# Attention and two expert layers on one core: a rewritten opening of the first batch, and attention work of every second step put ahead of the value product

## The chip, the cores and the metric

The kernel runs on one core of a Trainium2 chip. Its engines are TensorE (PE in the profile; its weight loads are PEld), VectorE (DVE), ScalarE (ACT), GpSimd (POOL) and SyncE (SP, which here issues nearly all DMAs). Each engine carries out its own instructions in the order in which the program writes them. The metric is device time in microseconds of one execution.

## The reference, cut to what matters

```python
# attention between x [8, 8, 512, 64] and state [8, 8, 32, 64], each way
a = softmax(x @ state.T / 8);   xread = a @ state      # 512 rows a batch
a2 = softmax(state @ x.T / 8);  sread = a2 @ x         # 32 rows a batch
x = rows of (xread, sread), heads side by side         # 4352 rows of 512
# gated layer
xn = x / sqrt(mean(x * x) + 1e-6) * rms_g
x = (silu(xn @ w_gate) * (xn @ w_val)) @ w_out         # 512 -> 1536 -> 512
# routed layer: rows with x @ w_skip > 0 go to the best of 8 experts
x[do] += gate * (relu(x[do] @ w1[e]) @ w2[e])          # 512 -> 1024 -> 512
```

## The kernel before, in words

**Passes and steps.** The gated layer runs in nine passes `b` over the rows: passes 0 to 7 take the 512 x-rows of one batch each, pass 8 the 256 state-rows. A pass has twelve steps `f`, one for each 128 of the 1536 inner columns. Float32 products are done as three products of a high and a low half (`mm3`, L844 to L846); the halves are made by a copy on ACT (L1024, L352) and a subtraction on DVE (L1025, L353).

A step goes: gate product `up(0, f)` into PSUM bank 4; tanh on ACT (L1374) and a multiplication on DVE (L1375), which reads the bank; value product `up(1, f)` into bank 5; a second multiplication on DVE (L1379), which reads that bank; the high half of h on ACT (L1382) and its low half on DVE (L1383); then the down product of the step before, four blocks of 128 rows into banks 0 to 3.

**Products with the states.** In passes 0 to 7 the first operand of the gate and value products is not the weight itself. As x is `a @ state`, the kernel multiplies the scaled states with the weights once for a pair of steps (`state_weights`, L331, eight products for each of two groups of heads) and uses the result with `a`, the attention's weights, as moving operand. These products are made in odd steps, halfway through the down product (`between`), into banks 4 and 5, and taken out as halves at L1024 and L1025. The group of bank 4 is written first. So they wait until L1375 and L1379 have read these banks, and the next step's gate and value products wait until L1024 and L1025 have.

**What fills the steps.** Attention of batch b+1, routing of batch b-1 and the preparation of weights (pass 0) are generators. A step has six places, `step(0)` to `step(5)`: 0 inside the gate product, 1 behind the gate's multiplication, 2 inside the value product, 3 behind the low half of h, 4 inside the down product, 5 behind it. A table gives the place (step, place) of each piece: `AT_FIRST` for the rest of batch 0, `AT_1` for batch 1, `AT` for batches 2 to 7, which run in passes 1 to 6, `AT_ROWS` for the routing in these passes. The order on each engine is thereby fixed when the program is written.

**The opening.** Batch 0 has no pass to run beside. Its code loads x and states, makes the scores (L389), the two softmaxes' pieces on DVE, ACT and POOL, reads of the states (L473, four products into banks 0 to 3), their squares (L521), the sums of the squares over heads by products with a column of ones (L527, one instruction pair for each 128 rows and group), the root (L532), its spread over partitions (L537), the multiplication by it (L539, L543), the halves, and the products with the states (L331); with `next(first)` all that is done ahead of pass 0. Between these stand copies, cuts and joins of the first weight units (`bits_w`, `cut_w`, `join_w`; the weights come as pairs of 32-bit words).

**Crossed loads.** The second group of heads keeps its even and odd heads in exchanged halves of the partitions (`half`, `crossed`), so that products of the two groups can use different rows of the array. A crossed tile takes two or three DMAs in place of one.

## Time and profile before

| | |
|---|---|
| median of 3 runs | 1151.21 us (1148.84 to 1153.84) |
| the profiled execution | 1153.5 us, its span 1151.7 us |
| opening, up to the first tanh of pass 0 | 0 to 41.9 us of the span |
| pass 0 (to the first tanh of pass 1) | 129.2 us |
| passes 1 to 6, each | 87.1 us (the last 86.1) |
| passes 7 and 8, routed layer | from 692.9 us |

Times inside the execution are read from the span's start. A row of the timeline gives start and length, so its end is their sum; an idle time in brackets is that of the engine ahead of the row, with what ended it. A row with a count is several equal instructions in turn. Lines (L1379) are those of the kernel before.

### The profile page before, as it was taken

The page shows a single profiled execution, that of the slowest core. Times are in us where ns is not written, and L with a number is a line of the kernel's source. Part 1 is how long each engine was busy: PE and PEld are TensorE (multiplying, and loading weights), DVE is VectorE, ACT ScalarE, POOL GpSimd, SP SyncE. Part 2 cuts the span into 40 slices and gives each one's busy share as a digit, 9 for nine tenths or more (in the row PEclk, how much of TensorE's full clock was granted, in tenths as well). Part 3 has the DMA queues.
Part 4 walks back from the last instruction along what each step waited for, and adds up shares of the span by engine and source line. Part 5 has one row for each costly group of instructions (what it writes and reads, how often), then busy time and mean ns, then how long its engine had stood idle before and what let it go on. Part 6 is the DMA issues. An engine that isn't in the chain of part 4 may idle for free. (4 is left out here: it accounts for less than half of the span.)

```text
span 1151.7 us, 16492 instructions
## 1 busy us (share of the span) xinstructions
PE 1053.3 (91%) x6110; PEld 788.0 (68%) x6110; DVE 713.6 (62%) x1412; ACT 475.7 (41%) x866; POOL 172.0 (15%) x160
## 2 busy tenths in 40 slices
PE   8686799999999999999999999999999979997964
PEld 5363556776776776776776777689878868786841
DVE  4778776776776776776776777667457343433321
ACT  3777653443443443443443444544315323332210
POOL 1353310010010010010010011532121130303020
PEclk8798799999999999999999999999999989998988
DMA  7866021021011012012012002015026533243230
GB/s 209 249 184 199 31 75 37 16 67 43 15 59 53 14 50 62 14 46 67 13 40 74 13 1 55 1 38 183 2 96 220 181 114 118 83 143 98 93 118 8
DMA packets 63638, 91.59 MB, mean 80 GB/s; under 512 B 16622, under 2 KB 38766, under 8 KB 63504
## 3 DMA queue, kind: packets, MB, share of 16 engines
q1 hardware_dynamic: 58288, 78.75, 22.2%
q0 software_dynamic: 5216, 11.18, 2.8%
q8 instruction: 69, 1.13, 0.4%
q14 instruction: 65, 0.53, 0.2%
HBM read 76.32 MB, written 15.81 MB: 80 GB/s over the span
## 5 line engine op out<-in xcount | busy, mean ns | idle before, releaser
L845 PE MATMUL ps<-w,hh 128*128 128x512 f32 x584 | 232.9, 399 | 23.3 <-DVE w L269 23.3
L844 PE MATMUL ps<-w,hh 128*128 128x512 f32 x584 | 238.7, 409 | 2.3 <-ACT nh L1024 1.8
L846 PE MATMUL ps<-w,hl 128*128 128x512 f32 x584 | 232.4, 398 | 0.7 <-DVE hl L1383 0.7
L845 PEld LDWEIGHTS ps<-w,hh 128*128 128x128 f32 x584 | 110.0, 188 | 49.7 <-DVE w L269 27.0
L844 PEld LDWEIGHTS ps<-w,hh 128*128 128x128 f32 x584 | 109.5, 188 | 45.6 <-issue 19.3
L1382 ACT ACTIVATE hh<-t 128x512 fp32r<-128x512 f32 (+1 forms) x108 | 65.6, 607 | 165.1 <-DVE t L1379 164.8
L846 PEld LDWEIGHTS ps<-w,hl 128*128 128x128 f32 x584 | 109.8, 188 | 28.0 <-DVE hl L1383 1.1
L836 POOL DMA_INDIRECT tlist<-lent,lidx x34 | 35.4, 1041 | 588.2 <-DVE lent L834 492.2
L1375 DVE SCALAR_TENSOR_TENSOR t<-t,ps 128x512 f32<-128x512 f32 (+1 forms) x108 | 70.1, 649 | 81.1 <-ACT t L1374 80.7
L1374 ACT ACTIVATE t<-ps 128x512 f32<-128x512 f32 (+1 forms) x108 | 61.8, 572 | 138.1 <-PE ps L846 136.9
L1383 DVE TENSOR_TENSOR hl<-t,hh 128x512 fp32r<-128x512 f32 (+1 forms) x108 | 76.9, 712 | 67.4 <-ACT hh L1382 67.3
L844 PE MATMUL ps<-nh,w 128*128 128x272 f32 (+2 forms) x320 | 104.0, 325 | 14.4 <-issue 13.0
L1022 DVE SCALAR_TENSOR_TENSOR hl<-ps,hh 128x272 fp32r<-128x272 f32 (+1 forms) x56 | 30.7, 548 | 123.0 <-ACT hh L1021 123.0
L845 PE MATMUL ps<-nl,w 128*128 128x272 f32 (+2 forms) x320 | 102.9, 322 | 0.0
L846 PE MATMUL ps<-nh,w 128*128 128x272 f32 (+2 forms) x320 | 102.9, 322 | 0.0
L1021 ACT ACTIVATE hh<-ps 128x272 fp32r<-128x272 f32 (+1 forms) x56 | 27.1, 483 | 160.2 <-PE ps L846 157.8
L844 PE MATMUL ps<-nh,xa 128*128 128x512 f32 x192 | 79.3, 413 | 11.2 <-DVE nl L1025 9.0
L1379 DVE SCALAR_TENSOR_TENSOR t<-t,ps 128x512 f32<-128x512 f32 (+1 forms) x108 | 70.7, 655 | 21.0 <-PE ps L846 14.1
L844 PE MATMUL ps<-nh 128*128 128x512 f32 x192 | 76.5, 398 | 4.4 <-DVE xa L1025 4.3
L844 PEld LDWEIGHTS ps<-nh,w 128*128 128x128 f32 x320 | 61.8, 193 | 21.4 <-issue 15.7
L845 PE MATMUL ps<-nl,xa 128*128 128x512 f32 x192 | 76.3, 397 | 0.0
L846 PE MATMUL ps<-nh,xa 128*128 128x512 f32 x192 | 76.3, 397 | 0.0
(240 smaller groups left out, 1823.4 us busy)
## 6 DMA issues: line engine op xcount, KB each, us to landing
w<-in_w_dram SPq DMA_DIRECT2D x52, 512.0 KB, 4.7
out_dram<-m SPq DMA_DIRECT2D x34, 256.0 KB, 3.8
m<-in_xN_dram SPq DMA_DIRECT2D x32, 256.0 KB, 3.4
w<-in_wo_dram SPq DMA_DIRECT2D x12, 512.0 KB, 7.8
m<-in_xT_dram SPq DMA_DIRECT2D x16, 256.0 KB, 3.5
m<-in_xT_dram SPq DMA_DIRECT2D x32, 128.0 KB, 2.7
w<-in_wg_dram SPq DMA_DIRECT2D x12, 256.0 KB, 4.9
w<-in_wv_dram SPq DMA_DIRECT2D x12, 256.0 KB, 5.1
```

The lines of the kernel that those rows point to most:

```text
L836: nc.gpsimd.indirect_dma_start(out=self.list, out_offset=bass.IndirectOffsetOnAxis(ap=self.idx[:, j:j + 1], axis=0), in_=self.ent[:, j], i ...
L844: mm(out, lhsT=ah, rhs=bh, start=first, stop=False)
L845: mm(out, lhsT=ah, rhs=bl, start=False, stop=False)
L846: mm(out, lhsT=al, rhs=bh, start=False, stop=last)
L1021: nc.scalar.activation(out=hi, in_=ps, func=AF.Relu)
L1022: nc.vector.scalar_tensor_tensor(lo, ps, 0.0, hi.bitcast(F32), ALU.max, ALU.subtract)
L1374: S.activation(out=t, in_=G, func=AF.Tanh, scale=0.5)
L1375: V.scalar_tensor_tensor(t, t, 1.0, G, ALU.add, ALU.mult)
L1379: V.scalar_tensor_tensor(t, t, 0.5, Vp, ALU.mult, ALU.mult)
L1382: S.activation(out=hh, in_=t, func=AF.Copy)
L1383: V.tensor_tensor(hl, t, hh.bitcast(F32), ALU.subtract)
```

## The change

**The opening.** For batch 0 the states and x are loaded uncrossed (one DMA for the states, four for x), and the scores of both groups use the same halves. A crossed copy of the states, the gains and the identity are loaded later, by `first_consts`, behind two weight units and the states' rows. The squares of the second and fourth read stay in PSUM, where they are; DVE adds them to the first and third, so there are two sums by products with ones and not four. The multiplied rows go to PSUM (`scaled_x`) and are split from there. The products with the states take banks 4 and 5. The first ends the code ahead of pass 0; the multiplication of the second rows, their halves and the second group's products with the states run inside the first gate product, which with its value product takes banks 2 and 3.

**The table.** In `AT` and `AT_ROWS`, pieces at place 3 of an odd step go to place 1; `take0` goes from place 3 to 5 of step 7; each of the four reciprocals goes one place ahead, the last from (11, 3) to (11, 1).

```diff
-AT = dict(... exp_s1=(1, 3), ... exp_n0=(3, 3), ... sums1=(5, 3), ... take0=(7, 3),
-          ... split=(9, 3), ... recip=((10, 3), (10, 5), (11, 0), (11, 3)), ...)
+AT = dict(... exp_s1=(1, 1), ... exp_n0=(3, 1), ... sums1=(5, 1), ... take0=(7, 5),
+          ... split=(9, 1), ... recip=((10, 1), (10, 3), (10, 5), (11, 1)), ...)
-AT_ROWS = dict(..., route=((2, 5), (7, 3), (8, 3), (9, 4), (9, 5)))
+AT_ROWS = dict(..., route=((2, 5), (7, 1), (8, 3), (9, 4), (9, 5)))
...
-        nc.sync.dma_start(out=self.ident, in_=ci)
-        self.crossed(self.g, g)
...
+    def first_consts(self, to, state):
+        ci, cu, cr, ct, c4, w9, g = self.consts
+        self.crossed(self.g, g)
+        self.crossed(to, state)
+        self.nc.sync.dma_start(out=self.ident, in_=ci)
...
     def attn_state(self, b):
-        self.crossed(self.stT, self.dstT[b])
+        if b:
+            self.crossed(self.stT, self.dstT[b])
+        else:
+            nc.sync.dma_start(out=self.stT, in_=self.dstT[b])
...
-            if g:
+            if g and b:
...
-                    p = self.half(g, q)
+                    p = self.half(g if b else 0, q)
...
             state()
+            crossed = self.tmp()
+            first_state = crossed[:, :128].rearrange("p (k n) -> p k n", n=32)
+            self.first_consts(first_state, self.dstT[0])
...
-            bits = [self.bits_w(*r) for r in raw[:2]]
+            bits = [self.bits_w(*raw[0]), self.bits_hi(*raw[1])]
...
-            q = [self.tmp() for _ in range(4)]
+            q = [self.tmp() for _ in range(2)]
             for k in range(4):
                 xread_start(k, xb[k])
-                S.activation(out=q[k], in_=xb[k], func=AF.Square)
+                S.activation(out=xb[k] if k % 2 else q[k // 2], in_=xb[k], func=AF.Square)
                 if k == 1:
+                    self.bits_lo(bits[1])
                     bits.append(self.bits_hi(*raw[2]))
-                for i in ((), (0,), (1,), (2, 3))[k]:
-                    for j in range(4):
-                        T.matmul(self.psb[4][:, j:j + 1], lhsT=q[i][:, j * 128:(j + 1) * 128], rhs=self.ones[:, 0:1], start=i == j == 0, stop=i == 3 and j == 3)
...
+            self.join_w(self.cut_w(bits.pop(0)))
             for i in range(2):
-                self.join_w(self.cut_w(bits.pop(0)))
+                V.tensor_tensor(q[i], q[i], xb[2 * i + 1], ALU.add)
+                for j in range(4):
+                    T.matmul(self.psb[4][:, j:j + 1], lhsT=q[i][:, j * 128:(j + 1) * 128], rhs=self.ones[:, 0:1], start=i == j == 0, stop=i == 1 and j == 3)
+            self.drop(*q)
+            self.join_w(self.cut_w(bits.pop(0)))
...
-            V.tensor_tensor(a1t[0], a1t[0], rr, ALU.mult)
-            self.xsplit_a1(a1t, 0)
-            self.join_w(self.cut_w(bits.pop(0)))
-            self.state_weights(0, self.psb[1:3], (0,))
-            V.tensor_tensor(a1t[1], a1t[1], rr, ALU.mult)
-            self.xsplit_a1(a1t, 1)
+            def rows(g):
+                V.tensor_tensor(scaled_x, a1t[g], rr, ALU.mult)
+                self.drop(a1t[g])
+                if g == 0:
+                    self.join_w(self.cut_w(bits.pop(0)))
+                self.halves(scaled_x, self.nh[:, g, :512], self.nl[:, g, :512])
+                self.state_weights(0, self.psb[4:6], (g,))
+
+            rows(0)
             S.activation(out=self.eps2, in_=self.eps, func=AF.Exp)
-            self.state_weights(0, self.psb[1:3], (1,))
+            yield 0, 0
+            rows(1)
...
-        out = self.psb[4 + k][:, :n]
+        out = self.psb[self.gv + k][:, :n]
...
+                self.gv = 2 if b == f == 0 else 4
                 G = self.up(0, f, n, lambda: step(0))
```

Three places in the order of the engines' instructions follow. Lines of the change are up to 21 higher than those before. The first is TensorE in the opening, from the reads of the states (L473, in the change L480) to the first value product. `ps_66` to `ps_69` are banks 0 to 3, `ps_70` and `ps_71` banks 4 and 5; the sums are L527 (L543), the products with the states L331 (L335). Before:

```order
L473 MATMUL ps_66<-m_225,m_151 128x512
L473 MATMUL ps_67<-m_225,m_151 128x512
L527 MATMUL ps_70<-ones,m_235 128x1 x4
L473 MATMUL ps_68<-m_233,m_151 128x512
L527 MATMUL ps_70<-ones,m_236 128x1 x4
L473 MATMUL ps_69<-m_233,m_151 128x512
L527 MATMUL ps_70<-ones,m_237 128x1 x4
L527 MATMUL ps_70<-ones,m_238 128x1 x4
L537 MATMUL ps_66<-ident,st_86 128x128 x4
L331 MATMUL ps_67<-w_216,sg 32x512 x4
L331 MATMUL ps_68<-w_244,sg 32x512 x4
L844 MATMUL ps_70<-nh,xa 128x512
```

and with the change:

```order
L480 MATMUL ps_66<-m_224,m_143 128x512
L480 MATMUL ps_67<-m_224,m_143 128x512
L480 MATMUL ps_68<-m_232,m_143 128x512
L480 MATMUL ps_69<-m_232,m_143 128x512
L543 MATMUL ps_70<-ones,m_234 128x1 x4
L543 MATMUL ps_70<-ones,m_235 128x1 x4
L551 MATMUL ps_66<-ident,st_86 128x128 x4
L335 MATMUL ps_70<-w_216,sg 32x512 x4
L863 MATMUL ps_68<-nh,xa 128x512
L864 MATMUL ps_68<-nl,xa 128x512
L865 MATMUL ps_68<-nh,xa 128x512
L335 MATMUL ps_71<-w_242,sg 32x512 x4
```

The four reads stand together, half of the sums are gone, and the second group's products with the states stand behind the first three gate products.

The second is DVE in step 5 of passes 1 to 6, from the first multiplication (L1375, in the change L1396) to the subtractions for the products with the states (L1025, L1044); L427 to L429 are `sums1`. Before:

```order
L1375 SCALAR_TENSOR_TENSOR t<-t,ps_70 128x512
L1379 SCALAR_TENSOR_TENSOR t<-t,ps_71 128x512
L1383 TENSOR_TENSOR hl_81<-t,hh_79 128x512
L427 TENSOR_REDUCE st_87<-m_1435 128x16
L428 TENSOR_SCALAR st_87<-st_87 128x16
L429 RECIPROCAL st_87<-st_87 128x16
L1025 TENSOR_TENSOR xa<-ps_70,xa 128x512
L1025 TENSOR_TENSOR xa<-ps_71,xa 128x512
```

and with the change:

```order
L1396 SCALAR_TENSOR_TENSOR t<-t,ps_70 128x512
L434 TENSOR_REDUCE st_87<-m_1427 128x16
L435 TENSOR_SCALAR st_87<-st_87 128x16
L436 RECIPROCAL st_87<-st_87 128x16
L1400 SCALAR_TENSOR_TENSOR t<-t,ps_71 128x512
L1404 TENSOR_TENSOR hl_81<-t,hh_79 128x512
L1044 TENSOR_TENSOR xa<-ps_70,xa 128x512
L1044 TENSOR_TENSOR xa<-ps_71,xa 128x512
```

The reduction, the addition and the reciprocal of `sums1` now stand between the two multiplications, and no longer ahead of the subtractions. Steps 1 (two instructions), 3 (two), 7 (five) and 9 (one) change in the same way, and step 11 with one reciprocal.

The third is ACT in step 7 of these passes, from the tanh to the next step's tanh (L1374, in the change L1395). L803 (L822) is the exponential of the routing, L486 (L493) are the squares of `take0`, L1024 (L1043) the copies of the products with the states, L466 (L473) parts of the next reads. Before:

```order
L1374 ACTIVATE t<-ps_70 128x512
L1382 ACTIVATE hh_79<-t 128x512
L803 ACTIVATE r_103<-r_102 128x32
L486 ACTIVATE m_1729<-ps_72 128x512
L486 ACTIVATE m_1731<-ps_73 128x512
L1024 ACTIVATE nh<-ps_70 128x512
L1024 ACTIVATE nh<-ps_71 128x512
L466 ACTIVATE m_1759<-m_1656 64x512
L466 ACTIVATE m_1762<-m_1656 64x512
L1374 ACTIVATE t<-ps_70 128x512
```

and with the change:

```order
L1395 ACTIVATE t<-ps_70 128x512
L822 ACTIVATE r_103<-r_102 128x32
L1403 ACTIVATE hh_79<-t 128x512
L1043 ACTIVATE nh<-ps_70 128x512
L1043 ACTIVATE nh<-ps_71 128x512
L493 ACTIVATE m_1747<-ps_72 128x512
L493 ACTIVATE m_1749<-ps_73 128x512
L473 ACTIVATE m_1754<-m_1648 64x512
L473 ACTIVATE m_1757<-m_1648 64x512
L1395 ACTIVATE t<-ps_70 128x512
```

The exponential moved ahead of the high half of h, and the two squares behind the copies.

## Rows read from the trace of the kernel before

**Rows 1.** Windows by stage: length, busy us and count by engine, granted clock, DMA share, GB/s.
```profile
16.55:37.04 20.49, 17.09 (x64) 9.74 (x60) 8.29 (x14) 10.07 (x17) 5.16 (x4) 0.55 0.88 248
...
258.25:345.38 87.13, 85.09 (x520) 61.70 (x519) 62.33 (x125) 36.43 (x65) 4.08 (x4) 1.00 0.14 42
```

**Rows 2.** TensorE's waits in the whole program: us in total, times, the longest.
```profile
PE ps L844 <- DVE nl L1025: 9.0, 12, 0.9
```

**Rows 3.** Timeline of the opening: start, length, engine, line, operation, count, idle time before.
```profile
1.37 3.36 PE L157 MATMUL ps<-ones 128*128 128x128 f32 x14 [1.37 <-DVE ones L139]
...
7.83 2.20 PE L389 MATMUL ps<-m,stT 64*32 64x512 f32 x8 [0.29 <-DMA m<-in_xT_dram]
...
16.86 0.71 DVE L443 STREAM_TRANSPOSE m<-m 128x512 f32<-128x512 f32 x1
...
23.14 2.07 PE L473 MATMUL ps<-m,m 64*128 64x512 f32 x2
...
25.14 3.57 PE L527 MATMUL ps<-ones,m 128*128 128x1 f32 x16
...
31.39 0.69 DVE L539 TENSOR_TENSOR m<-m,ps 128x512 f32<-128x512 f32 x1 [1.74 <-PE ps L537]
...
35.27 1.92 PE L331 MATMUL ps<-w,sg 64*32 64x512 f32 x4 [2.04 <-POOL w L251]
...
39.49 0.40 PE L844 MATMUL ps<-nh,xa 128*128 128x512 f32 x1
...
39.72 0.39 PE L845 MATMUL ps<-nl,xa 128*128 128x512 f32 x1
...
41.88 0.57 ACT L1374 ACTIVATE t<-ps 128x512 f32<-128x512 f32 x1
...
47.91 0.61 ACT L1382 ACTIVATE hh<-t 128x512 fp32r<-128x512 f32 x1
```

**Rows 4.** DMA issues of the first 13 us: KB each, median us to landing.
```profile
m<-in_stN_dram SPq DMA_DIRECT2D x1, 256.0 KB, 5.5
```

**Rows 5.** Timeline, pass 2, step 1 to the first product of step 2.
```profile
264.98 0.69 DVE L1379 SCALAR_TENSOR_TENSOR t<-t,ps 128x512 f32<-128x512 f32 x1
...
265.40 1.41 PE L331 MATMUL ps<-w,sg 64*32 64x512 f32 x16
...
266.97 0.68 DVE L395 TENSOR_REDUCE st<-ps 128x1 f32<-128x512 f32 x1
...
269.92 0.50 PE L844 MATMUL ps<-nh 128*128 128x512 f32 x1 [0.54 <-DVE xa L1025]
```

**Rows 6.** Timeline, pass 2, step 3 to the first product of step 4.
```profile
279.50 0.69 DVE L1379 SCALAR_TENSOR_TENSOR t<-t,ps 128x512 f32<-128x512 f32 x1
...
280.76 1.09 PE L331 MATMUL ps<-w,sg 64*32 64x512 f32 x16
...
282.21 0.69 DVE L412 TENSOR_TENSOR m<-m,st 128x512 f32<-128x512 f32 x1
...
284.82 0.50 PE L844 MATMUL ps<-nh,xa 128*128 128x512 f32 x1 [0.56 <-DVE nl L1025]
```

**Rows 7.** Timeline, pass 2, step 5: the states' products.
```profile
294.72 1.57 PE L331 MATMUL ps<-w,sg 64*32 64x512 f32 x16
```

**Rows 8.** Timeline, pass 2, step 7 to the first product of step 8.
```profile
308.21 0.69 DVE L1379 SCALAR_TENSOR_TENSOR t<-t,ps 128x512 f32<-128x512 f32 x1 [1.01 <-PE ps L846]
...
311.08 0.19 DVE L806 TENSOR_REDUCE r<-r 128x4 f32<-128x32 f32 x1
...
313.11 0.49 PE L844 MATMUL ps<-nh,xa 128*128 128x512 f32 x1 [0.94 <-DVE nl L1025]
```

**Rows 9.** Timeline, pass 2, step 11.
```profile
336.19 0.69 DVE L1379 SCALAR_TENSOR_TENSOR t<-t,ps 128x512 f32<-128x512 f32 x1
...
337.20 1.09 PE L331 MATMUL ps<-w,sg 64*32 64x512 f32 x16
...
338.19 0.94 DVE L674 RECIPROCAL m<-m 128x128 f32<-128x128 f32 x1
```

More of the change, by code (lines that the diff above doesn't have):

```diff
@@ L43 @@
             a1_1=(9, 0), xread1=(9, 4), take1=(9, 5), sum=(10, 0), split=(10, 1), ones=(10, 4), root=(10, 5), recip=((11, 0), (11, 1), (11, 2), (11, 3)), scale=(12, 0))
-AT = dict(scores=(0, 0), exp_s0=(0, 2), flip0=(0, 5), exp_s1=(1, 3), flip1=(1, 5), scale_s0=(2, 3), scale_s1=(2, 5), exp_n0=(3, 3), turn=(3, 4),
-          copy0=(3, 5), copy1=(4, 3), scaled0=(4, 5), sums1=(5, 3), sread=(5, 4), scaled1=(5, 5), parts=(6, 3), a1_0=(6, 5), xread0=(7, 2), take0=(7, 3),
-          a1_1=(7, 5), xread1=(8, 2), take1=(8, 3), sum=(8, 5), split=(9, 3), ones=(9, 4), root=(9, 5), recip=((10, 3), (10, 5), (11, 0), (11, 3)), scale=(12, 0))
-AT_ROWS = dict(turn=(0, 3), parts=(0, 5), logits=(1, 4), lt=(1, 5), lq=(2, 4), route=((2, 5), (7, 3), (8, 3), (9, 4), (9, 5)))
+AT = dict(scores=(0, 0), exp_s0=(0, 2), flip0=(0, 5), exp_s1=(1, 1), flip1=(1, 5), scale_s0=(2, 3), scale_s1=(2, 5), exp_n0=(3, 1), turn=(3, 4),
+          copy0=(3, 5), copy1=(4, 3), scaled0=(4, 5), sums1=(5, 1), sread=(5, 4), scaled1=(5, 5), parts=(6, 3), a1_0=(6, 5), xread0=(7, 2), take0=(7, 5),
+          a1_1=(7, 5), xread1=(8, 2), take1=(8, 3), sum=(8, 5), split=(9, 1), ones=(9, 4), root=(9, 5), recip=((10, 1), (10, 3), (10, 5), (11, 1)), scale=(12, 0))
+AT_ROWS = dict(turn=(0, 3), parts=(0, 5), logits=(1, 4), lt=(1, 5), lq=(2, 4), route=((2, 5), (7, 1), (8, 3), (9, 4), (9, 5)))
 AT_ROWS_LAST = dict(AT_ROWS, route=((2, 5), None, None, (3, 4), (3, 5)))
@@ L343, in attn_state, with scaled_state @@
         self.stT = self.sp.tile([128, 4, 32], F32, tag="stT", name="stT", bufs=1)
-        self.crossed(self.stT, self.dstT[b])
-    def scaled_state(self):
+        if b:
+            self.crossed(self.stT, self.dstT[b])
+        else:
+            nc.sync.dma_start(out=self.stT, in_=self.dstT[b])
+    def scaled_state(self, state=None):
         self.sg = self.sp.tile([128, 4, 32], F32, tag="sg", name="sg", bufs=1)
-        self.nc.vector.tensor_tensor(self.sg, self.stT, self.g.unsqueeze(2).to_broadcast([128, 4, 32]), ALU.mult)
+        self.nc.vector.tensor_tensor(self.sg, self.stT if state is None else state, self.g.unsqueeze(2).to_broadcast([128, 4, 32]), ALU.mult)
     def halves_sb(self, x, hi, lo):
@@ L512, in attn @@
             back(0)
-            self.scaled_state()
+            self.scaled_state(first_state)
+            self.drop(crossed)
             sums(1)
@@ L534, in attn @@
             bits.append(self.bits_w(*raw[3]))
-            rr = xb[0]
+            rr, scaled_x = xb[:2]
             for j in range(4):
```

2 lines of the change are left out of this document (1 added, 1 removed).

## The prediction

> **What bounds the kernel now.** I read the windows by stage first, then TensorE's waits, then the timeline of one pass step by step, and of the first 50 us. From pass 1 to pass 6 every pass repeats itself to a few hundredths: 87.13 us, of which PE is busy 85.09, DVE 62.33 and ACT 36.43, at the full clock [rows 1]. So TensorE is the bound there, and only its waits can be taken away. It has three of size in a pass, ahead of the first product of steps 2, 4 and 8, that is, behind the odd steps 1, 3 and 7: 0.54, 0.56 and 0.94 us [rows 5, 6, 8]; the second and third, which wait for a low half in `nl`, are 12 waits and 9.0 us over six passes [rows 2]. A product that waited starts 0.17 later than its listed gap says, since matmul records overlap (0.40 long, 0.23 apart [rows 3], at 39.49 and 39.72): counted in starts, the three cost 0.70, 0.72 and 1.11. That is 2.5 us a pass, 15 us in six passes, the most that the new table can bring. Ahead of them the opening is different: from 16.55 to 37.04 TensorE is granted 0.55 of its clock [rows 1], and the stretch is one chain through four engines, with the first tanh at 41.88 [rows 3].
>
> **The table.** An odd step on DVE is: gate's second multiplication (L1375), value's (L1379), low half of h (L1383), attention work, then the subtractions for the states' products (L1025). PE issues the states' products (L331) halfway through the down product. They write the banks of gate and value, so the first may start after L1375 and the second after L1379. The change puts the attention work between L1375 and L1379: the subtractions come earlier, the second of the states' products may come later. Step by step:
>
> Step 1. L1379 ends at 265.67, and the states' products, begun at 265.40, take 1.41 instead of 1.09 [rows 5, 6]: the second already waits 0.32 for it. The reduction (0.68) and a small instruction (0.15, partly covered) move ahead: L1379 starts 0.60 later, and so does all behind it on PE. The next gate product could then start at 269.22+0.60 = 269.82 (269.22 is where it stood without a wait); now it starts at 269.92 [rows 5]. Gain 0.10, not 0.70: the wait moves from one product to the other.
>
> Step 3. L1379 (279.50) is pushed back by a reduction and a subtraction (0.69, ending at 282.90 behind a low half that ended at 281.57), so by 1.4 less the 0.25 it has of slack: it ends at 281.34. The states' products start at 280.76, so the second waits 0.62. The next product moves to 284.10+0.62 = 284.72, against 284.82 [rows 6]. Gain 0.10.
>
> Step 5. Nothing waits in front of step 6, so there is nothing to win. L331 takes 1.57 here [rows 7], 0.48 of it a wait for L1379. A reduction and two instructions of 16 columns (0.68, 0.2 and 0.2) would add 0.9 if nothing else changed. But DVE runs one unbroken chain from step 3's subtractions through step 4 to here, and the first of those ends at 282.47 (end of the states' products) + 0.6 + 0.69 = 283.8 now, where the product behind it waited until 284.82 [rows 6]. Loss between 0.9 and nothing; I take 0.1, since I find no idle time in that chain, and so nearly all of the lead arrives.
>
> Step 7. The five routing instructions (0.19 for the last, which ends at 311.27; 1.0 together) go where DVE waits 1.01 for PE anyway, because two state reads stand inside the value product: L1379 stays at 308.21 [rows 8]. `take0`'s two squares no longer stand on ACT before the copies of the states' products. These then begin when PE is done, the subtraction ends at about 312.0, and the wait of 1.11 is gone. Behind it step 8's parts come late by up to 0.15. Gain 0.95 to 1.1; I take 1.05.
>
> Step 9: a split of the sums, one subtraction, goes ahead of L1379, which by my count still ends just before the states' products start: nothing, at worst 0.1. Steps 10 and 11: four reciprocals move one place ahead each; the last (0.94) now stands before step 11's L1379, which moves from 336.19 to about 336.8. Its states' products start at 337.20, so they wait 0.3 [rows 9], and no wait was there to be won. Loss 0.3 (0.2 to 0.4).
>
> Sum: 0.10+0.10-0.10+1.05-0.30 = 0.85 gained a pass, rounded to 0.8; in six passes 4.9 us. The unfavourable ends give -0.2 a pass, the best 2.5.
>
> **The opening.** (a) Five whole loads stand where nine stood. The warming products end at 4.73, and scores of 2.0 to 2.2 us each [rows 3] with x there in time end at 8.75 instead of 10.03. DVE's chain behind them, which ends at 17.57 [rows 3], ends at 16.3. (b) Before, the third and fourth read of the states stood apart, each 2.07 at the lower clock, with sums between; the last 16 instructions of the sums took 3.57 and ended at 28.71 [rows 3]. Now both reads start at 16.3 side by side (they use different rows of the array) and end at 18.4, two squares of 0.6 end at 19.6, an addition of 0.69 at 20.35, and the last eight sum instructions, at half of 3.57, at 22.2. That is 6.5 earlier, the largest piece. (c) Root, reciprocal and the spreading products keep their 2.7 us: the first multiplication by the root moves from 31.39 to 25.0. (d) From there to the first tanh ACT and DVE have the same instructions, less PE's wait of 2.04 ahead of L331 [rows 3], but the second rows now follow a table load on ACT. From 25.0: multiplication, high and low half, copy and subtraction of the first states' products, five instructions of 0.6 to 0.7, to 28.3; multiplication and high half of the second rows to 29.7; their states' products, 1.92 at the lower clock [rows 3], to 31.6; a copy to 32.2; five weight copies of 0.65 on ACT, which stood here before too, to 35.5. That is where the tanh starts, 6.3 earlier. (e) The first exponential of the scores stood ahead of this tanh and now stands behind it; it needs the multiplication (0.69) and a reduction and a small one (0.85), which themselves follow the tanh, so ACT idles 1.6 and then does 0.9. From tanh to the first high half of h it was 6.0 us (41.88 to 47.91 [rows 3]); now 8.3. Net 4.0 us earlier. Bounds: 6.3 if that idle time is hidden later, 2 if (d) or the loads disappoint. The rest of pass 0 has no wait of ACT's weight copies for a transfer, so I let it move along whole.
>
> What is moved behind it on SP's queue: gains, crossed states and the identity now follow two weight units and the states' rows. The transfer in that place took 5.5 us to land [rows 4]; issued by 8.9, the crossed states land between 12.2 and 14.4. Scaled states, first user on DVE, stand at 13.5: late by 0 to 0.9, inside the bounds.
>
> Multiplying into PSUM and splitting from there I price at nothing: a DVE instruction on SBUF alone took 0.69 (L412 [rows 6]), one with a PSUM operand 0.69 (L539 [rows 3]). [...]
>
> **Sum.** The profiled execution took 1153.5 us: 1153.5 - 4.0 - 4.9 = 1144.6. The median of the runs shown is 2.3 lower, 1151.2, so 1142.3 is what I forecast for a median; 0.5% (5.8 us) is about what a measurement here can tell from no change.
>
> **Rivals.** (A) The second states' product takes back all that the table wins: the unfavourable ends, step 5's 0.9 above all, -0.2 a pass. For it: steps 1 and 5 show that very wait already. Against it: DVE is ahead by then. Time 1151.2-4.0+1.2 = 1148.4. (B) The waits go and no new ones come, 15 us: 1151.2-4.0-15 = 1132. Against it: L1379 is at the edge in steps 1, 3, 5 and 11. (C) The opening's lead is lost again in pass 0, where ACT and DVE are loaded; the table alone: 1151.2-4.9 = 1146.3. (D) Slower: gains, crossed states and identity land late behind the weights. Scaled states stand in DVE's order ahead of the second group's sums, so all behind waits. Each us of landing past 13.5 costs one; the opening's gain is gone at 17.5, all of it at 22.4, and slower by 0.5% needs 28. Against it: the 5.5 us of [rows 4]. (E) The clock: PE ran at 0.55 until 37.04 [rows 1], with holes like the 2.04 before L331, which then took 1.92 for the second rows [rows 3], against 1.09 for both groups at the full clock [rows 6]. With up products from 28 on and a shorter hole, the clock could return sooner; the second half's states' products would then take about 1 us less, 1141.3. [...]
>
> **How the numbers follow.** Chances: forecast 0.52, its own range 1138 to 1146; A 0.16, B 0.06, C 0.13, D 0.03, E 0.10. The time is the forecast's. The range leaves out B, D and the slow end of A: 1137 to 1148. Faster by over 0.5% means under 1145.4: most of the forecast (0.48), B, E, and the lucky part of A and C (0.08 together), 0.72. Within 0.5%: the rest of those three, 0.24. Slower: D and what I overlook, 0.04.
>
> **What would show it.** Right: the first high half of h near 44, passes of about 86.3, no wait before step 8, waits before steps 2 and 4 gone but L331 longer in steps 1, 3 and 11 (1.7 to 2.0, 1.7, 1.4). Wrong: passes at 87 with L331 over 2.3 in step 5 (A), passes near 84.7 (B), the first tanh early but pass 1 beginning as late as now (C), DVE idle before the scaled states (D).

## The result, and the profile after

The change took 1137.31 us (median of 4 runs, 1135.86 to 1138.83) against 1150.03 for the kernel before: ratio 0.9885, 95% interval 0.9855 to 0.9915. A second set of runs (change_again) gave 1136.86 against 1151.36, ratio 0.9878 (0.9853 to 0.9903). So it is 13 to 14 us faster, where 8.9 were forecast. The direction and the two sources were right; both were larger, the opening most of all.

Windows of the change (columns as in [rows 1]): the same stretch of the opening, and pass 2.

```profile
16.55:37.04 20.49, 16.00 (x62) 9.19 (x58) 11.16 (x23) 13.62 (x25) 7.45 (x6) 0.67 0.99 261
247.77:333.80 86.03, 86.03 (x520) 62.05 (x519) 61.71 (x125) 36.74 (x65) 4.18 (x4) 1.00 0.15 40
```

A pass is 1.09 us shorter, and TensorE is now busy in all of it: of the row `nl` of [rows 2] (12 waits, 9.0 us) one wait of 0.8 us is left, in pass 0. That "busy" is not all work, as the next rows show. Timeline of pass 2 with the change: steps 1, 3, 5, 7 and 11 (L335 the states' products, L1400 the value's multiplication; [rows 5 to 9] answer to them).

```profile
254.31 0.68 DVE L402 TENSOR_REDUCE st<-ps 128x1 f32<-128x512 f32 x1
254.92 1.99 PE L335 MATMUL ps<-w,sg 64*32 64x512 f32 x16
255.09 0.68 DVE L1400 SCALAR_TENSOR_TENSOR t<-t,ps 128x512 f32<-128x512 f32 x1
...
270.00 1.75 PE L335 MATMUL ps<-w,sg 64*32 64x512 f32 x16
...
283.78 1.74 PE L335 MATMUL ps<-w,sg 64*32 64x512 f32 x16
...
297.45 0.69 DVE L1400 SCALAR_TENSOR_TENSOR t<-t,ps 128x512 f32<-128x512 f32 x1
...
298.73 1.09 PE L335 MATMUL ps<-w,sg 64*32 64x512 f32 x16
...
324.11 0.94 DVE L693 RECIPROCAL m<-m 128x128 f32<-128x128 f32 x1
...
325.51 1.23 PE L335 MATMUL ps<-w,sg 64*32 64x512 f32 x16
```

Each of these rows is eight products, four for each group of heads, and each product is two records. `state_weights` makes them by turns, one of the group of bank 4 and one of the group of bank 5; the text ahead of the prediction counts eight for each group and has bank 4's group first, which is not so. So only the first product can start ahead of L1400. The same row of step 1, cut off at 255.8:

```profile
254.92 1.04 PE L335 MATMUL ps<-w,sg 64*32 64x512 f32 x2
```

L1400 ends at 255.78, and the other fourteen records start behind it. The row that needs 1.09 us takes 1.99, 1.75, 1.74 and 1.23 where the reduction or the reciprocal stands ahead of L1400: the wait is inside the row, behind its first product, and no idle time in brackets shows it. Only in step 7 did a wait go without a new one.

Timeline of the opening with the change (answers to [rows 3]): scores, third and fourth read, sums, multiplication by the root, second states' products, first tanh, first exponential of the scores, first high half of h.

```profile
4.65 3.18 PE L396 MATMUL ps<-m,stT 64*32 64x512 f32 x16
...
15.72 1.74 PE L480 MATMUL ps<-m,m 64*128 64x512 f32 x4 [1.88 <-DVE m L450]
...
17.39 3.82 PE L543 MATMUL ps<-ones,m 128*128 128x1 f32 x16
...
23.89 0.70 DVE L555 TENSOR_TENSOR ps<-m,ps 128x512 f32<-128x512 f32 x1 [1.74 <-PE ps L551]
...
28.01 1.90 PE L335 MATMUL ps<-w,sg 64*32 64x512 f32 x8
...
33.44 0.57 ACT L1395 ACTIVATE t<-ps 128x512 f32<-128x512 f32 x1
...
35.55 0.69 ACT L405 ACTIVATE m<-ps,st 128x512 f32<-128x512 f32 x1 [1.54 <-DVE st L403]
...
40.87 0.63 ACT L1403 ACTIVATE hh<-t 128x512 fp32r<-128x512 f32 x1
```

The first tanh stands 8.4 us earlier (41.88 before), the first high half of h 7.0 (47.91). The span fell by 15.3: 7.0 there, 2.3 in the rest of pass 0, 6.65 in passes 1 to 6 (521.78 to 515.13), less 0.7 behind them.

### The profile page after: what moved, and what is told of

Read it like the earlier page. It is cut to its first block, busy times and chain, and to the rows that moved or that the text cites. A ratio compares the mean times of both kernels' runs of the same rounds, so it can differ in the third digit from the quotient of the medians.

```text
span 1136.4 us, 16433 instructions
## 1 busy us (share of the span) xinstructions
PE 1055.6 (93%) x6094; PEld 787.7 (69%) x6094; DVE 710.7 (63%) x1414; ACT 477.8 (42%) x866; POOL 170.7 (15%) x160
## 3 DMA queue, kind: packets, MB, share of 16 engines
q8 instruction: 69, 1.13, 0.5%
## 5 line engine op out<-in xcount | busy, mean ns | idle before, releaser
L864 PE MATMUL ps<-w,hh 128*128 128x512 f32 x584 | 234.1, 401 | 22.2 <-DVE w L273 20.2
L864 PEld LDWEIGHTS ps<-w,hh 128*128 128x128 f32 x584 | 110.5, 189 | 49.1 <-DVE w L273 23.9
L1396 DVE SCALAR_TENSOR_TENSOR t<-t,ps 128x512 f32<-128x512 f32 (+1 forms) x108 | 70.1, 649 | 95.2 <-ACT t L1395 94.9
L1395 ACT ACTIVATE t<-ps 128x512 f32<-128x512 f32 (+1 forms) x108 | 61.9, 573 | 145.3 <-PE ps L865 145.1
L1404 DVE TENSOR_TENSOR hl<-t,hh 128x512 fp32r<-128x512 f32 (+1 forms) x108 | 76.6, 710 | 68.4 <-ACT hh L1403 68.4
L335 PE MATMUL ps<-w,sg 64*32 64x512 f32 x768 | 74.1, 635 | 2.1 <-DVE t L1400 1.3
L865 PE MATMUL ps<-nh,nl 128*128 128x512 f32 x192 | 75.7, 395 | 0.0
```

The lines of the kernel that those rows point to most:

```text
L335: self.nc.tensor.matmul(banks[g][32 * q:32 * q + 32, :], lhsT=self.sg[p, k, :], rhs=self.U[F, k].bitcast(F32)[p, :], start=True, stop=True)
L864: mm(out, lhsT=ah, rhs=bl, start=False, stop=False)
L865: mm(out, lhsT=al, rhs=bh, start=False, stop=last)
L1395: S.activation(out=t, in_=G, func=AF.Tanh, scale=0.5)
L1396: V.scalar_tensor_tensor(t, t, 1.0, G, ALU.add, ALU.mult)
L1404: V.tensor_tensor(hl, t, hh.bitcast(F32), ALU.subtract)
```

## The experiments

The table has all results: medians against the runs of before on the same chip, and what the profile of each shows (one execution each). "First h" is the start of the first high half of h; "lower clock" is the first stretch of the opening in which TensorE was granted half of its clock (0.50), from the trace's clock records (later ones are left out); "rest" is from first h to the first tanh of pass 1.

| kernel | median, before | ratio (95%) | first tanh | first h | lower clock | rest of pass 0 |
|---|---|---|---|---|---|---|
| before | | | 41.88 | 47.91 | 18.6-39.0 | 123.17 |
| table_alone | 1144.47, 1151.99 | 0.9934 (0.9916-0.9952) | 41.44 | 47.50 | 19.5-33.2 | 121.23 |
| step_seven_alone | 1147.80, 1151.99 | 0.9949 (0.9929-0.9969) | 43.32 | 49.36 | 18.4-42.3 | 121.67 |
| before_cuts | 1152.30, 1151.75 | 1.0007 (0.9991-1.0023) | 39.48 | 45.53 | 21.2-34.9 | 121.35 |
| before_warm | 1147.97, 1151.75 | 0.9971 (0.9957-0.9985) | 38.99 | 45.05 | 23.1-30.0 | 119.63 |
| late_constants | 1149.63, 1152.05 | 0.9984 (0.9971-0.9997) | 41.31 | 47.37 | 18.8-32.4 | 119.72 |
| change | 1137.31, 1150.03 | 0.9885 (0.9855-0.9915) | 33.44 | 40.87 | 16.1-29.8 | 120.87 |
| change_again | 1136.86, 1151.36 | 0.9878 (0.9853-0.9903) | 33.65 | 41.12 | 17.0-30.6 | 121.48 |
| opening_alone | 1141.87, 1151.99 | 0.9903 (0.9884-0.9921) | 33.10 | 40.59 | 16.1-29.7 | 121.23 |
| other_places | 1128.91, 1151.99 | 0.9796 (0.9772-0.9819) | 31.84 | 39.29 | 19.4-33.1 | 121.53 |
| crossed_loads | 1138.07, 1149.76 | 0.9898 (0.9877-0.9919) | 35.24 | 42.70 | 18.3-28.6 | 121.35 |
| four_sums | 1137.82, 1149.76 | 0.9901 (0.9882-0.9920) | 34.63 | 42.09 | 17.5-27.7 | 121.03 |
| loads_and_sums_back | 1140.82, 1151.36 | 0.9910 (0.9886-0.9935) | 37.24 | 44.73 | 21.5-38.5 | 121.80 |
| old_cuts | 1136.85, 1151.75 | 0.9878 (0.9856-0.9900) | 33.62 | 41.08 | 16.5-26.8 | 121.20 |
| early_constants | 1138.15, 1152.05 | 0.9877 (0.9858-0.9896) | 33.12 | 40.57 | 16.6-26.9 | 121.32 |
| rows_ahead | 1135.31, 1149.76 | 0.9872 (0.9848-0.9896) | 31.26 | 38.74 | 15.5-25.7 | 121.49 |
| exponential_first | 1136.41, 1151.36 | 0.9866 (0.9841-0.9891) | 33.18 | 39.21 | 19.8-33.5 | 121.87 |
| warm_holes | 1134.18, 1149.76 | 0.9859 (0.9842-0.9875) | 31.95 | 39.42 | 19.8-26.6 | 122.69 |
| combined | 1126.80, 1151.36 | 0.9780 (0.9756-0.9804) | 32.56 | 40.01 | 20.6-30.8 | 122.88 |
| both_best | 1128.64, 1151.75 | 0.9798 (0.9779-0.9816) | 32.63 | 38.66 | 15.7-29.4 | 121.95 |

Before, table_alone and step_seven_alone have one opening: first h at 48.26 in the mean, within 1.9 us of each other. The change, change_again, opening_alone and other_places have the new one: 40.47 in the mean, within 1.8. So the opening gained 7.8 us, and a difference of under 2 us between two single profiles of the opening cannot be told from none.

### The two halves of the change apart

**table_alone** (the kernel before with the table of the change), **opening_alone** (the change with the table of before).

> The kernel before with the change's table of places and nothing else. By the prediction's terms (0.8 a pass): 4.9 us faster than before, a pass of 86.3 us. By the trace of the change (passes of 86.03, six of them 6.7 us shorter): 6.6 us faster, and the opening of pass 0 as before (first tanh at 41.9, first high half of h at 47.9). Rival: the table needs the earlier opening to gain anything, as DVE is later without it; then less than 2 us, and passes of over 86.8.

> The change with the old table. By the prediction's terms: 4.0 us faster than before. By the trace of the change, first high half of h at 40.9 where 47.9 stood: 7.0 us faster. Two theories of the further 2.3 us that pass 0 lost between its step 1 and pass 1: (i) they are the clock of the one profiled execution of before, 2.3 us above its median; then pass 0 from the first high half on differs by its stretches at the lower clock alone, and the time is 7.0 below before; (ii) they belong to the earlier opening, and come again: 9.3 below before. Passes 1 to 6 stay at 87.1 each.

Windows of pass 2, first table_alone:

```profile
254.72:340.74 86.02, 86.02 (x520) 62.06 (x519) 61.75 (x125) 36.74 (x64) 4.30 (x4) 1.00 0.14 41
```

and opening_alone:

```profile
249.00:336.12 87.12, 85.07 (x520) 61.69 (x519) 62.36 (x125) 36.41 (x64) 4.33 (x4) 1.00 0.13 41
```

The table brings its 1.1 us a pass without the new opening (515.26 for passes 1 to 6), so that rival falls. The rest of pass 0 is 121.2 us in both, with the old opening and with the new: the 123.17 of the profiled execution of before was its own, theory (i). (Single executions differ here: two variants of the old opening, before_warm and late_constants, have 119.6 and 119.7.) The medians say more than the traces for the opening: 11.2 us (9.1 to 13.4) against 7.3 up to first h. The two halves then add to 18.8 where the change has 14.0; these few us are not explained.

**step_seven_alone** (the kernel before with two edits):

```diff
-... take0=(7, 3), ... route=((2, 5), (7, 3), ...)
+... take0=(7, 5), ... route=((2, 5), (7, 1), ...)
```

> The kernel before with only the two edits of step 7 (the squares behind the copies, the routing's reduction ahead of the value's multiplication). By the prediction's term 1.05 a pass, 6.3 us; by the trace of the change 0.96 a pass, 5.8 us: then all the other edits of the table together bring only the rest, under 1 us in six passes. Rival: step 7's gain comes in part from attention work that reached it earlier; then under 4 us, and the wait before step 8 stays at half its size.

Its window of pass 2:

```profile
257.17:343.33 86.16, 85.07 (x520) 61.61 (x519) 62.37 (x125) 36.53 (x64) 4.25 (x4) 1.00 0.14 42
```

0.96 a pass, 5.2 us in six (516.56; two passes were 0.3 to 0.4 longer than the others). All other edits of the table bring 1.3.

### Where the rest of the table's gain is

**other_places** (the change with the pieces of steps 1, 3, 5 and 11 out of the way of L1400):

```diff
-... exp_s1=(1, 1), ... exp_n0=(3, 1), ... sums1=(5, 1), ... recip=((10, 1), (10, 3), (10, 5), (11, 1)), ...
+... exp_s1=(1, 5), ... exp_n0=(3, 0), ... sums1=(5, 5), ... recip=((10, 0), (10, 1), (10, 3), (10, 5)), ...
```

> The change with four more pieces moved: in step 1 the reduction behind the subtractions for the states' products, in step 3 the reduction and subtraction ahead of the gate's multiplication, in step 5 the sums behind the subtractions, in steps 10 and 11 each reciprocal one place ahead, so that nothing stands between the gate's and the value's multiplication in steps 1, 3, 5 and 11. If the states' products wait there for the value's multiplication alone (1.99, 1.75, 1.74 and 1.23 us in place of 1.09), each falls to 1.09, a pass is 2.3 us shorter (83.7), and the kernel 14 us faster than the change: 1123. Rival: these waits only cover the next one; the gate product of steps 2, 4 and 6 then waits for the subtraction again, with passes at 85.5 or more and less than 4 us gained. Second rival: the exponential ahead of step 3's tanh delays the tanh, and step 3 gives back up to 0.6 a pass.

The states' products of its steps 1, 3 and 5 (timeline; in step 3 with the gate's and value's multiplications ahead of them), and its pass 2 (windows):

```profile
252.58 1.41 PE L335 MATMUL ps<-w,sg 64*32 64x512 f32 x16
...
265.86 0.69 DVE L1400 SCALAR_TENSOR_TENSOR t<-t,ps 128x512 f32<-128x512 f32 x1 [1.19 <-ACT t L1399]
266.65 0.69 DVE L1404 SCALAR_TENSOR_TENSOR t<-t,ps 128x512 f32<-128x512 f32 x1
267.06 1.42 PE L335 MATMUL ps<-w,sg 64*32 64x512 f32 x16
...
280.53 1.09 PE L335 MATMUL ps<-w,sg 64*32 64x512 f32 x16
```

```profile
245.44:330.00 84.56, 84.56 (x520) 61.63 (x519) 62.31 (x125) 36.78 (x65) 3.88 (x4) 1.00 0.14 39
```

The waits were for the value's multiplication, and no wait of size came back ahead of steps 2, 4 and 6: 1.47 us more a pass, 8.5 in six, and the median 23 us below before. The expected 14 were too many, as 1.09 is only reached in steps 5 and 11: in steps 1 and 3 the value's multiplication (L1404 here) itself ends 0.3 us behind the start of the states' products, in step 3 behind a tanh for which DVE waits 1.19, in step 1 behind copies and a transpose that DVE does without a pause. Another 0.25 a pass was lost in steps 6 and 7 (5.56 to 5.63 and 8.00 to 8.18 from tanh to tanh).

### The parts of the opening, taken out of the change

**crossed_loads** (first diff; the states are loaded crossed too), **four_sums** (second diff; the additions and the two sums behind the reads left out) and **loads_and_sums_back** (both):

```diff
-            if g and b:
+            if g:
...
-                    p = self.half(g if b else 0, q)
+                    p = self.half(g, q)
```

```diff
-S.activation(out=xb[k] if k % 2 else q[k // 2], in_=xb[k], func=AF.Square)
+S.activation(out=q[k], in_=xb[k], func=AF.Square)
...
+for i in ((), (0,), (1,), (2, 3))[k]:
+    for j in range(4):
+        T.matmul(self.psb[4][:, j:j + 1], lhsT=q[i][:, j * 128:(j + 1) * 128], ...)
```

> The change with x and states of the first batch loaded crossed again (nine loads in place of five). By the prediction's step (a), 1.3 us later up to the end of the transposes (17.0 where the change has 15.66) and 1.3 us slower in all; by the two traces, where the scores of the second group end 2.2 us earlier with the change (7.83 against 10.03), 1.9 to 2.2 us. Rival: nothing, as the first high half of h stands behind weight copies on ACT that do not depend on x.

> The change with all four squares in SBUF and four sums by products between the reads, as before. By the prediction's step (b), 5.2 us later at the root (6.5 less the 1.3 of the loads); by the two traces (from the last transpose to the last sum 5.6 now, 11.1 before) 5.6. First high half of h then at 46, against 40.9, and the kernel 5 us slower than the change. Rival: part of the 11.1 us was the lower clock, begun at another moment; then 3 or less.

> The change with both the crossed loads and the four sums of before. Each alone put the first high half of h at 42.7 and 42.1, where the change's opening gave 40.9, 40.6 and 39.3 (mean 40.3): 2.4 and 1.8 later. If the two add, 44.5 here, and half of the 8 us between the openings is in other parts (the order of the weights' cuts, the late constants, the places of multiplication and split). If each alone was covered by the other's slack, both together give nearly all: 46.5 to 48.

Against 40.47, undoing the loads costs 2.2 us, the sums 1.6, both 4.3. That looks like a sum, with 3.5 of the 7.8 elsewhere, but each is one profile, good to some 2 us. By the medians both together cost 3 to 4 us (0.9910 against 0.9885 and 0.9878), and the intervals overlap. The sums disappoint: undone alone they move the root's multiplication by 2.8 (26.70 against 23.89), not by 5.2. TensorE in four_sums:

```profile
15.97 1.12 PE L480 MATMUL ps<-m,m 64*128 64x512 f32 x2
17.02 1.50 PE L538 MATMUL ps<-ones,m 128*128 128x1 f32 x8
18.45 2.07 PE L480 MATMUL ps<-m,m 64*128 64x512 f32 x2
```

The third read and the sums behind it took 1.12 and 1.50, most of it ahead of the lower clock (from 17.5), where the old opening took 2.07 and 1.86. So the 5.2 were a price of the sums and of the clock together.

**rows_ahead** (the second rows ahead of pass 0; the exponential keeps its place), and **exponential_first** (ahead of the first tanh):

```diff
-            yield 0, 0
             rows(1)
...
-lanes.append([(x for p in (first, rest()) for x in p), (0, 0), 1])
+lanes.append([(x for p in (first, rest()) for x in p), (0, 1), 1])
```

```diff
             A = AT_FIRST
-            yield A["exp_s0"]
             exp_s(0)
```

> The change with the second rows and their products with the states ahead of the first gate product again, all else as it is (the first exponential stays behind the tanh). If the deferral gains what the three gate products take that then lie under the second rows' work, the first tanh is 1.0 to 1.6 us later than 33.4. If ACT decides (its five weight copies end at 33.58, just ahead of the tanh), the second states' products only start 1.5 us sooner, and tanh and time stay within 0.5 us.

> The change with the first exponential of the scores ahead of the first tanh, as before. By the prediction's step (e) its place behind the tanh costs 2.3 us up to the first high half of h, of which 1.4 come back here once the exponential's own 0.9 us is counted; by the trace ACT idles 1.54 us behind the tanh for it. So tanh 0.9 later, first high half of h 1.4 to 1.5 us earlier, and the kernel as much faster. Rival: the time is made good again in steps 0 and 1 anyway, as their weight copies fill ACT; then pass 1 starts no earlier.

Neither part of the change is seen to bring anything. With the second rows ahead, first h came at 38.74, 1.7 earlier; with the exponential ahead, the tanh to h took 6.03 us again, not 7.43, and first h came at 39.21, 1.3 earlier; both are inside the 2 us that two profiles of one opening differ by. Both medians lie 0.1% under the change's, which the intervals do not tell from none. What the deferred second rows cost stands on ACT, in its copy of the second states' products: first the change, where TensorE makes them behind three gate products, then rows_ahead.

```profile
29.99 0.60 ACT L1043 ACTIVATE xa<-ps 128x512 fp32r<-128x512 f32 x1 [1.61 <-PE ps L335]
```

```profile
27.86 0.59 ACT L1042 ACTIVATE xa<-ps 128x512 fp32r<-128x512 f32 x1
```

The five weight copies and the tanh follow this copy on ACT in both.

**warm_holes**: 13 products of ones added in TensorE's holes.

```diff
 if k == 1:
+    self.warm(8)
...
 rr, scaled_x = xb[:2]
+self.warm(2)
...
+self.warm(3)
 S.activation(out=self.eps2, in_=self.eps, func=AF.Exp)
```

> The change with 13 idle products added in TensorE's three holes of the opening: 8 between the second and third read of the states (hole of 1.88 us, products of 0.24), 2 ahead of the spread of the root (0.57), 3 ahead of the first gate product (0.72). If the lower clock from 16.1 to 29.75 comes from these holes, it stays away or comes later, and the reads, sums, spread and states' products there take about 4 us less: first tanh at 30 to 31. Rival: the clock falls all the same, and the added products stand in the way: tanh at 33.4 to 35.

The lower clock came 2.8 to 3.7 us later than in the change, change_again and opening_alone, and stayed for 6.8 us, not 13.7; but in other_places, with no products added, it began as late, at 19.4. The third and fourth read took 1.13 in place of 1.74 (in other_places too), and the tanh came 1.1 us ahead of the mean of the four (33.0), not 3. Once the clock was low, the idle products stood in the way: the root's spread started 0.34 us behind the reciprocal that it waits for (21.07 to 21.41), in the change 0.05.

### What the open 3.5 us are

**before_warm** (the kernel before with 11 idle products), **before_cuts** and **old_cuts** (the order of the first weight units' work put into before, and taken out of the change).

```diff
-            self.warm(20)
+            self.warm(26)
...
 if k == 1:
+    self.warm(3)
...
 rr = xb[0]
+self.warm(2)
```

```diff
-bits = [self.bits_w(*r) for r in raw[:2]]
+bits = [self.bits_w(*raw[0]), self.bits_hi(*raw[1])]
...
 if k == 1:
+    self.bits_lo(bits[1])
...
-self.xsplit_a1(a1t, 0)
 self.join_w(self.cut_w(bits.pop(0)))
+self.xsplit_a1(a1t, 0)
```

> The kernel before with 11 idle products in the holes of its opening: 6 ahead of the first read of the states (hole of 1.41 us), 3 ahead of the first sums (0.79), 2 ahead of the root's spread (0.56). If the lower clock from 18.6 on is what makes up the open 3.5 us, the third and fourth read take 1.1 in place of 2.07 each and the sums between them 1.05 in place of 1.87: the root's multiplication 2.7 to 4 us earlier (27.4 to 28.7 against 31.39) and the first high half of h at 44 to 45. If the order of the weights' cuts is, the root's multiplication moves by under 1 us.

> The kernel before with the change's order of weight work alone: the second half of the second unit's bits behind the second square, and the fourth unit's cut ahead of the first rows' split. By the traces, the first square then starts up to 0.9 us earlier (behind the transpose, not behind four weight copies), and TensorE's 2.04 us wait for the fourth unit goes: first high half of h 1.5 to 3 us earlier (45 to 46.5). If the clock is the cause of the open 3.5 us: under 1 us, but for a shift of the stretch at the lower clock.

> The other side of it: the change with the order of weight work of before (both units' bits ahead of the squares, both joins behind the sums, the fourth unit's cut behind the first rows' split). If that order makes up the open 3.5 us, first high half of h at 43 to 44 against 40.5; if the clock does, within 1 us of 40.5.

Before_warm, timeline: the reads of the states and the sums between them (answers to [rows 3], 23.14 and 25.14).

```profile
18.65 1.02 PE L528 MATMUL ps<-ones,m 128*128 128x1 f32 x8
19.60 1.12 PE L473 MATMUL ps<-m,m 64*128 64x512 f32 x2
20.66 1.05 PE L528 MATMUL ps<-ones,m 128*128 128x1 f32 x8
21.64 1.12 PE L473 MATMUL ps<-m,m 64*128 64x512 f32 x2
...
28.69 0.69 DVE L541 TENSOR_TENSOR m<-m,ps 128x512 f32<-128x512 f32 x1 [1.87 <-PE ps L539]
```

Without a change of its work, the old opening does its reads in 1.12 instead of 2.07, its sums in 1.05 instead of 1.86, and the root's multiplication stands at 28.69 instead of 31.39. The kernel is 3.3 us faster (1.7 to 5.0 by the interval of the medians; the profile is the fastest of its ten runs and shows more). The order of the cuts is worth nothing that shows in either direction (1.0007; 0.9878, the change's own ratio). The profile of before_cuts, the fastest of its ten runs, shows first h at 45.53, and in it the lower clock begins at 21.2 instead of 18.4 to 19.5: a single execution can have this with a median that is no faster.

Loads_and_sums_back, the change's text with the very reads and sums of before, had them at the full clock too:

```profile
18.33 1.12 PE L477 MATMUL ps<-m,m 64*128 64x512 f32 x2
19.38 1.05 PE L535 MATMUL ps<-ones,m 128*128 128x1 f32 x8
20.36 1.12 PE L477 MATMUL ps<-m,m 64*128 64x512 f32 x2
```

Two reads of 1.12 for 2.07 and sums of 1.05 for 1.86 are 2.7 of the 3.5 between this profile and the old opening: in these executions the open part is in the main the clock. That any edit of the change puts the lower clock off is not shown. In the change itself it begins earlier (16.1), in the middle of its last two reads (1.74), and its sums, its spread and its states' products run at it. By the medians the open part is 2.8 us (0.9910 against 0.9934 for table_alone), with intervals that overlap.

**late_constants** (before, with identity and gains loaded behind the states' rows) and **early_constants** (the change, with both ahead of the weights):

```diff
-nc.sync.dma_start(out=self.ident, in_=ci)
-self.crossed(self.g, g)
...
 state()
+nc.sync.dma_start(out=self.ident, in_=self.consts[0])
+self.crossed(self.g, self.consts[6])
```

> The kernel before with identity and gains loaded behind the states' rows and two weight units, and nothing else. The states' rows are then issued 2.3 us earlier (8.2 against 10.4). If their landing (15.97, 0.14 ahead of the first read) made the hole ahead of the first read, that hole of 1.41 us falls under 0.4, the first read starts at 14.9 to 15.2, and the kernel is 1 to 3 us faster, by as much as the stretch at the lower clock is shorter. If the first read only waited with the rest of the chain (DVE's second transpose at 16.86, ACT's squares at 17.39 behind four weight copies), nothing moves: within 1 us.

> The change with identity and gains loaded ahead of the weights again, as before; the crossed states stay where the change put them. The states' rows are issued at 7.4 in place of 5.1 and land at 12.9 by the 5.5 us that the transfer took before, 0.2 behind the first read of the change (12.71): first high half of h within 0.5 us of 40.5. If the constants' place was worth 2 us or more by itself, 42.5 or later, through the weights that land 2.3 us later too.

Late_constants, timeline of TensorE in the same place:

```profile
15.43 1.13 PE L471 MATMUL ps<-m,m 64*128 64x512 f32 x4 [0.19 <-DVE m L441]
17.79 1.05 PE L527 MATMUL ps<-ones,m 128*128 128x1 f32 x8 [1.23 <-ACT m L521]
18.77 2.07 PE L471 MATMUL ps<-m,m 64*128 64x512 f32 x2
```

The hole ahead of the first read did come from the states' rows: 1.41 became 0.19. But the next one, in which the first sums wait for ACT's square, grew from 0.79 to 1.23, and the lower clock began at 18.8, as in the old opening. That is 1.8 us (0.3 to 3.3) in the median. In the change the same edit gives nothing (0.9877).

### Versions that beat both kernels

**change_again** is the change once more; **combined** is other_places with rows_ahead and the first 10 of the idle products of warm_holes; **both_best** is other_places with rows_ahead and exponential_first.

> The change itself once more, for the runs of this chip and a second profile. The opening's time has differed between executions of one text (first high half of h at 40.9 and, with the same opening, at 40.6 and 39.3; before 47.9, 47.5 and 49.4). Expected from these: 39.3 to 40.9 again, passes 1 to 6 at 515.1, and 13 us faster than before.

> The other places of the table, the second rows ahead of the first gate product, and 10 idle products in TensorE's two first holes, together. By what each brought up to the end of the part that it touches (passes 1 to 6: 8.5 us; first high half of h 1.5 to 2.1 and 0.9 to 1.5 earlier): 11 to 12 us faster than the change, 1126. If the two edits of the opening only moved the clock's lower stretches, their gains do not add: 9 us, 1128, the same as the other places alone.

> The change with the other places of the table, the second rows ahead of the first gate product and the first exponential ahead of the first tanh: the three edits that each made the change faster by themselves, without idle products. If they add (8.5, 1.7 and 1.3 us): 11 to 12 us faster than the change, 1125, with the first high half of h at 37.5. If the two of the opening share one cause (ACT's queue ahead of the tanh), 38.5 and 1126 to 1127.

All three with the other places are 2.0 to 2.2% faster than before, some 9 to 11 us faster than the change. What was added to the opening is lost in them: first h at 40.01 and 38.66, against 39.29 for other_places, and ratios 0.9780 and 0.9798 against 0.9796. The best measured is combined, 1126.80, but its interval does not set it apart.

## Why the prediction was right or wrong

**The sum.** 4.0 + 4.9 was forecast; in the two profiles compared it was 7.0 + 6.65. The step that failed is the opening's net of 4.0. The mechanism, a shorter chain up to the first high half of h, was right, but three of its terms were about 1 us too small each: up to the root's multiplication (6.4 forecast, 7.5 measured), from there to the tanh (10.5 forecast, 9.55 measured), and the exponential's new place (a loss of 2.3 forecast, 1.4 measured).

**The table** was right in mechanism and 1.75 us too small. Step 7: 1.05 forecast, 0.97 measured from tanh to tanh (8.97 to 8.00), and 0.96 a pass alone. Step 1: 0.10, measured 0.24 (8.96 to 8.67, of which step 2 gives back 0.05). Steps 3 and 5 together: 0, measured 0.02; step 3 wins 0.91 and steps 4 and 5 lose 0.68 and 0.21. Step 11: -0.30, measured -0.12, as its states' products take 1.23, not the 1.4 forecast. The states' products of steps 1, 3 and 5 (1.7 to 2.0, 1.7, "under 2.3") came as forecast at 1.99, 1.75 and 1.74. So "the wait moves from one product to the other" held, and rival A was wrong in its size alone. What was overlooked is that this wait can be avoided, by places on the other side of the two multiplications: 8.5 us.

**The opening, step by step.** (a) The loads: 1.3 forecast; the second transpose ended at 15.66 where 16.3 was forecast, 1.9 earlier than before, and undoing the loads cost 2.2. (b) The sums: forecast to end at 22.2, they ended at 21.21, 7.5 earlier than before with the loads' part; 0.6 of this 1.0 is (a), 0.3 the two reads, which took 1.74 and not 2.1. (Two reads on different halves of the partitions did run side by side: at the full clock two took 1.13 together in late_constants, one took 1.12 in before_warm.) But undone by themselves the sums cost 1.6 to 2.8, not 5.2: the rest of the difference between the two traces is the clock, at which the old reads ran, and the forecast put it down to the sums. (c) The root's multiplication: 25.0 forecast, 23.89. (d) From there to the tanh: 10.5 forecast, 9.55. The second states' products took 1.90 (1.92 forecast), but they did not wait for the second rows' high half, as the forecast had it: they started at 28.01, and it ended at 28.38, behind a table load on ACT that took 1.28 (26.40). That is 0.5. The weight copies between them and the tanh took 2.85 us and not 3.3, as ACT's records overlap (0.67 to 0.79 long, 0.56 to 0.64 apart). (e) The exponential behind the tanh: 2.3 forecast as lost, 1.4 measured (tanh to h 6.03 to 7.43, an idle ACT for 1.54 of it), and 1.3 came back when it was undone. The forecast added ACT's new idle time and did not see an old one go, that of the second exponential, here before and with the change:

```profile
44.33 0.69 ACT L398 ACTIVATE m<-ps,st 128x512 f32<-128x512 f32 x1 [0.77 <-DVE st L396]
```

```profile
37.33 0.67 ACT L405 ACTIVATE m<-ps,st 128x512 f32<-128x512 f32 x1
```

(d) and (e) say rightly that these two parts bring nothing. That the sums of (b) came out within 1 us is in part luck: the forecast priced both chains at the lower clock; this one profile of before had its last two reads and all behind them there, and the change fell to it at 16.1, ahead of nearly all that was priced.

**Rival E** did not come as it was put: the clock came back at 29.8, not at 39.0, but the second states' products ended only then and still took 1.90, where a microsecond less was its sign. That a shorter hole brings the clock back sooner was the author's estimate: with the old opening's holes filled (before_warm) the lower clock lasted 6.9 us, in before 20.5, but in table_alone, with the holes as they were, 13.7. What E left out is that the old opening's own reads and sums ran at half the clock (2.07 and 1.86 against 1.12 and 1.05 in before_warm). Filling the holes of the old opening gives 3.3 us without any of the change's edits, so the clock there is worth about what was open. How much of the change's own gain is the clock stays open, and so does why the clock falls at 16 us in one execution and at 21 in another. Late constants alone gave 1.8 us and the order of the cuts alone nothing; the two together were not tried.

**The other rivals.** B (all waits go, 15 us) was the nearest in size to what a better table can do (6.65 and 8.5 with other_places), not to this one. C is refuted: the rest of pass 0 is as long with the lead as without. D is refuted: the scaled states waited 0.16 us for their transfer, and the queue's order was, if anything, a gain. The 2.3 us from the profiled execution to the median fit in size the rest of pass 0, 123.17 there and 121.2 to 121.7 in table_alone, step_seven_alone and before_cuts; no run shows more of it.

**PSUM operands** were free in these forms, as priced: the multiplication into PSUM took 0.70 (L555), the one into SBUF 0.69 [rows 3]; the subtraction behind it that reads PSUM took 0.69 (L1044, at 25.25), the one that reads SBUF 0.69 (L353 before, at 32.77).

## What to carry to other kernels

A wait that is moved into the middle of a group of matmuls shows no idle time, only a longer row (here 1.99 us for 1.09): compare each group's duration with its shortest one before calling TensorE busy. Where two readers of PSUM stand on one engine and products wait for both, keep other work ahead of the first or behind the second, not between them (here 8.5 us, other_places). In a stretch that is a chain through several engines, price each step at both clock levels (here 1.12 or 2.07 for a read), and take several profiles before giving a part of it a number under 2 us.

## What the runs showed of the hardware that was not expected

TensorE's lower clock began, in the same place of the same opening, at 16.1, 16.1, 17.0 and 19.4 us in four executions of the new one, and lasted 13.6 to 13.7 us in each; with the old one it began at 18.4 to 19.5 and lasted 13.7, 20.5 and 23.9. Ahead of the fall, TensorE had groups of products with holes between them, none over 1.9 us in the change (1.88 ahead of its third read). So the moment of the fall differed by up to 3.3 us between executions of one opening. At the lower level (0.50 of the clock) a read took 2.07 us against 1.12, the sums of a read (eight records) 1.86 against 1.05, a group's products with the states (eight records) 1.90 against 1.06 in four_sums. A median over runs holds all of these; a single profile holds one.
